# Four output half rows straight from the accumulator instead of two, with the accumulator copied out by two engines and the last left group moved behind the last right product

## The chip, the cores and the metric

The kernel runs on 1 core of one Trainium2 chip. The metric is the device time of one execution in microseconds. Before the change it is 201.84 us, the median of 3 runs (201.77 to 201.89).

## The reference

Two stages follow each other. A slot attention over 8 batches and 8 heads makes `x`; a soft mixture of 8 experts with 4 slots each (32 slots in all) makes the output, 4608 rows of 512 columns.

```python
logits = x @ phi                       # 4608 x 32
d = softmax(logits, over rows)         # dispatch
slot_input = d.T @ x                   # 32 slots
for e in range(8):                     # 4 slots an expert
    slot_out[e] = relu(slot_input[e] @ w1[e]) @ w2[e]
c = softmax(logits, over slots)        # combine
out = c @ slot_out                     # 4608 x 512
```

The change touches only the last two lines: how `slot_out` is gathered from its accumulator, and how `out` is multiplied, evicted and stored.

## The kernel before

Every operation of the kernel is entered with `add(engine, cost, ...)` in a plan. `Plan.order` then plays the plan through with the given costs and issues the operations in the order in which they would start; so the order of each engine's instructions comes from those costs, from the tiles' dependencies and from the `after` lists.

**The expert weights.** `expert_in` (line 1385) multiplies the slot inputs by `w1`, `hidden` applies the relu (line 1401, ScalarE) and transposes (line 1410, TensorE; line 1416, VectorE), `mult` (line 1431) multiplies by `w2`. The second product is kept in two accumulators, one for each half of the 512 output columns: the left half in `kvbank`, the right half in `scbank`. In each, four groups of 32 partitions hold four partial sums. The last four half experts' `w2` come in quarter loads of 256 KB, left columns first (`tail_out`). The four left products of these tails (`tail_mult(0, n)`) therefore end before the four right ones (`tail_mult(1, n)`).

**The slot sums.** `slot_sums(d)` copies the accumulator of half `d` to `accs` (tile name `cS`, line 1349; VectorE for the left half, ScalarE for the right one), multiplies it by `rep`, which adds the four partial sums (line 1357), and splits the sum in a high part (ScalarE cast, line 1364) and a low part (VectorE subtraction, line 1369): the two halves of `sr`.

**Output rows.** The combine weights `c` are transposed to `cT`, also as high and low parts. `out_mult` (line 1603) makes 128 output rows of a batch pair with two matmuls of 64 rows, one for each part. `direct` (line 1587) needs no slot sums: it multiplies `accs` itself by `c4`, four copies of the transposed weights one under the other, in one full fp32 matmul. The copies in `c4` are made by ScalarE (line 1553), in the middle of `slots(0)`. Each product goes to one of four PSUM banks and is evicted to SBUF, by ScalarE (line 1579) or VectorE (line 1580).

**Order of the end.** The left half is written out by four groups of three half rows while the right products still run; `RIGHT = (-1, 1, 2, 2)` says behind which left group each right tail product stands. Then come the right slot sums, four right groups, and at last 24 products of the full 512 columns, stored as 3, 3, 9 and 9 rows. All stores and loads are issued by SyncE (stores on line 1616), 16 stores in this order: left half rows 0, 1, 2 one by one, left groups 1, 2, 3, the same six for the right half, and the four wide stores.

Of the kernel before, what the change touches and what calls it, by code (L numbers as in the profile page):

```python
# [16 lines left out]
PE, DVE, ACT, POOL, SP = range(5)  # L17
# [3 lines left out]
class Plan:  # L21
# [24 lines left out]
    def add(self, eng, cost, fn, r=(), w=(), also=(), pri=None, dma=0.0, slack=0.0, after=()):  # L46
        cost, ni = cost if isinstance(cost, tuple) else (cost, 4)
        i = len(self.ops)
        deps = set()
        tiles = {}  # L50
        for x in r:
            for key in x:
                tiles[key[0]] = None
                if key in self.last_w:
                    deps.add(self.last_w[key])
        for x in w:
            for key in x:
                tiles[key[0]] = None
                if key in self.last_w:
                    deps.add(self.last_w[key])  # L60
                deps.update(self.reads.get(key, ()))
        for x in w:
            for key in x:
                self.last_w[key] = i
                self.reads[key] = []
        for x in r:
            for key in x:
                self.reads.setdefault(key, []).append(i)
        deps.discard(i)
        deps.update(after)  # L70
        tiles = [t for t in tiles if t.pool is not None]
        for t in tiles:
            t.users += 1
        need = tiles + [t for t in also if t not in tiles]
        if pri is None:
            pri = self.phase[0]
            self.phase[0] += self.phase[1]
        self.ops.append((eng, cost, fn, deps, pri, dma, tiles, need, slack, ni))
        return i
# [170 lines left out]
def dve(n):  # L250
    return 0.15 + n / 960.0


def act(n, psum=True):
    return (0.16 if psum else 0.19) + n / 1200.0
# [15 lines left out]
def kernel(  # L271
# [30 lines left out]
    P = 128  # L302
# [40 lines left out]
    Q_SZ, QT_SZ = C * J * D, C * J * D // 2  # L343
    KP_W = R * (P + Y)
    EX_SZ = PC + JN
    ARENA = 44288
    arena = const.tile([P, ARENA], F32, name="arena")

    CT_ALL = NBP * J * P
    TOP = 10 ** 6  # L350
    top_pool = ExitStack()
    qtile = top_pool.enter_context(tc.tile_pool(name="top", bufs=1)).tile([P, CT_ALL], F32, name="top")
# [943 lines left out]
        [qtile[:, i * W_SZ: i * W_SZ + W_SZ] for i in range(2)],  # L1296
        [(TOP + i * W_SZ, W_SZ) for i in range(2)], [qs],
    )
    ND = 2
    late_tiles = []  # L1300

    def late(x, off, n):
# [35 lines left out]

    pacc = [b_kv.tile(), b_s2.tile()]
    HD = DM // 2  # L1340
    accs = acs.tile().split(2)
    sr = keep("sr", [P, 2, DM], dtype=F32R, parts=2)
    so = [b_l.tile(), Tile(ap=kvbank[:, 1])]

    def slot_sums(d, middle=lambda: None):
        x = slice(d * HD, d * HD + HD)
        add(
            *((ACT, act(HD)) if d else (DVE, dve(HD))),
            lambda: (nc.scalar.copy if d else nc.vector.tensor_copy)(
                accs.ap[:, x], pacc[d].ap[:, 0, :HD]  # L1350
            ),
            r=[pacc[d]], w=[accs.part(d)],
        )
        y = middle()
        z = add(
            PE, 0.5,
            lambda: nc.tensor.matmul(
                so[d].ap[:, :HD], rep.rearrange("p a n -> p (a n)"), accs.ap[:, x],
                start=True, stop=True,
            ),  # L1360
            r=[accs.part(d), rep_b], w=[so[d]], after=[y] if y is not None else (),
        )
        add(
            ACT, act(HD), lambda: nc.scalar.copy(sr.ap[:, 0, x], so[d].ap[:, :HD]),
            r=[so[d]], w=[sr.part(d)],
        )
        add(
            DVE, dve(HD),
            lambda: nc.vector.tensor_tensor(
                sr.ap[:, 1, x], so[d].ap[:, :HD], sr.ap[:, 0, x].bitcast(F32), op=ALU.subtract  # L1370
            ),
            r=[so[d], sr.part(d)], w=[sr.part(d)],
        )
        return z
# [123 lines left out]
    def slots(bp):  # L1498
        Lb = L[bp]
        lv = Lb.ap.rearrange("p (j n) -> p j n", j=J)  # L1500
        mx, sm = cmxs.tile(), csms.tile()
        cxb, cx = Lb, lambda: lv
        bc = lambda t: t.ap.unsqueeze(2).to_broadcast([P, J, NS])
        add(
            DVE, dve(JN), lambda: nc.vector.tensor_reduce(mx.ap, lv, axis=AX.X, op=ALU.max),
            r=[Lb, SIM], w=[mx],
        )
        add(
            DVE, dve(JN),
            lambda: nc.vector.tensor_tensor(cx(), lv, bc(mx), op=ALU.subtract),  # L1510
            r=[mx], w=[cxb],
        )
        add(ACT, act(JN, False), lambda: nc.scalar.activation(cx(), cx(), AF.Exp), r=[cxb], w=[cxb])

        def f():
            nc.vector.tensor_reduce(sm.ap, cx(), axis=AX.X, op=ALU.add)
            nc.vector.tensor_scalar(sm.ap, sm.ap, EPS, None, op0=ALU.add)
            nc.vector.reciprocal(sm.ap, sm.ap)
            nc.vector.tensor_mul(cx(), cx(), bc(sm))

        add(DVE, 1.2, f, r=[cxb], w=[sm, cxb])
        x, ct = xs.tile().split(2), cTs.tile().split(2)
        cT[bp] = ct
        for a in range(2):
            js = range(a, J, 2)
            n, h = len(js) * P, HALF * a

            def f(a=a, h=h, n=n):
                o = x.ap[h: h + NS, :n].rearrange("m (j q p) -> m q j p", q=4, p=NS)
                for i in range(4):  # L1530
                    nc.vector.transpose(o[:, i], cx()[NS * i: NS * i + NS, a::2, :])

            add(DVE, 4 * dve(n // 4), f, r=[cxb], w=[x.part(a)])
            add(
                ACT, act(n, False),
                lambda h=h, n=n: nc.scalar.copy(ct.ap[h: h + NS, :n], x.ap[h: h + NS, :n]),  # L1536
                r=[x.part(a)], w=[ct.part(a)],
            )
            add(
                POOL, pool_tt(n),  # L1540
                lambda h=h, n=n: nc.gpsimd.tensor_tensor(  # L1541
                    ct.ap[h + NS: h + HALF, :n], x.ap[h: h + NS, :n],
                    ct.ap[h: h + NS, :n].bitcast(F32), op=ALU.subtract,
                ),
                r=[x.part(a), ct.part(a)], w=[ct.part(a)],
            )
        if bp == 0:

            def f():
                for i in range(ND):  # L1550
                    h = HALF * i
                    for y in range(0, P, NS):
                        nc.scalar.copy(c4.ap[y: y + NS, i * P: i * P + P], x.ap[h: h + NS, :P])

            add(ACT, 4 * ND * act(P, False), f, r=[x], w=[c4])

# [24 lines left out]
        )  # L1581

    def direct(d, i, after=()):
        po, ot, s = b_o.tile(), half[0], slice(d * HD, d * HD + HD)
        x = add(
            PE, 0.45,
            lambda: nc.tensor.matmul(
                po.ap[:, :HD], c4.ap[:, i * P: i * P + P], accs.ap[:, s],
                start=True, stop=True,
            ),  # L1590
            r=[accs.part(d), c4], w=[po], also=[ot], after=after,
        )
        add(
            *evict(lambda: ot.ap[:, i * DM + s.start: i * DM + s.stop], po, HD, i % 2 == d),
            r=[po], w=[ot.part(G * d + i)],
        )
        store(0, i, s, ot, [ot.part(G * d + i)], i)
        return x

    def out_mult(bp, j, po, x):  # L1600
# [19 lines left out]
            r=r, dma=P * n * (x.stop - x.start) * 4 / (DMA_RATE if x.stop - x.start == DM else HALF_RATE),  # L1620
        )

    def half_group(d, n, single=False):
        (bp, j0), ot, x = groups[n], half[n], slice(d * HD, d * HD + HD)
        for i in range(ND if single else 0, G):
            po = b_o.tile()
            z = add(
                PE, 0.22, lambda po=po, j=j0 + i: out_mult(bp, j, po, x),
                r=[sr.part(d), cT[bp]], w=[po], also=[ot],
            )  # L1630
            y = i * DM + d * HD
            add(
                *evict(lambda y=y: ot.ap[:, y: y + HD], po, HD, (j0 + i) % 2),
                r=[po], w=[ot.part(G * d + i)],
            )
            if single:
                store(bp, j0 + i, x, ot, [ot.part(G * d + i)], i)
        if not single:
            store(bp, j0, x, ot, [ot.part(G * d + i) for i in range(G)])
        return z  # L1640

    outv = out.rearrange("(p j) d -> p j d", j=J)
    z = slot_sums(0)
    for i in range(ND):
        z = direct(0, i, [z])
    for n in range(-1, NA):
        if n >= 0:
            z = half_group(0, n, n == 0)
        for m in range(NT):
            if RIGHT[m] == n:  # L1650
                tail_mult(1, m, [z])
        if RIGHT[NT - 1] == n:
            y = slot_sums(1)
            for i in range(ND):
                y = direct(1, i, [y])
    for n in range(NA):
        half_group(1, n, n == 0)
    for bp, j0, n in ((1, 3, 3), (1, 6, 3), (2, 0, 9), (3, 0, 9)):
        ot = (ots if n == G else big[n]).tile().split(n)
        for i in range(n):  # L1660
# [42 lines left out]
```

## Time and profile before

| what | value |
|---|---|
| median of 3 runs | 201.84 us |
| the profiled execution | 201.61 us |
| its span, first to last instruction | 199.8 us |
| TensorE busy | 168.4 us (84%), 2595 matmul records |
| VectorE busy | 140.7 us (70%) |
| ScalarE busy | 74.0 us (37%) |
| GpSimd busy | 95.5 us (48%) |
| DMA | 76.47 MB, mean 383 GB/s |

The rest of the execution, 1.8 us, lies outside of the span. The page shows the span in 40 slices of 5 us: DMA is at nine tenths or more in nearly all of them, and moves 396 to 431 GB/s in most of the later ones; in the seven slices from 160 us on it moves 313, 337, 303, 238, 369, 417 and 413 GB/s, and 295 in the last. The granted TensorE clock is at its upper level until 193 us. An fp32 matmul has two records in the trace, so one `tail_mult` of four matmuls is shown as x8, and one `direct` as x2; one `out_mult` is x2 as well.

### The profile page before, as it was taken

The page shows a single profiled execution, that of the slowest core. Times are in us where ns is not written, and L with a number is a line of the kernel's source. Part 1 is how long each engine was busy: PE and PEld are TensorE (multiplying, and loading weights), DVE is VectorE, ACT ScalarE, POOL GpSimd, SP SyncE. Part 2 cuts the span into 40 slices and gives each one's busy share as a digit, 9 for nine tenths or more (in the row PEclk, how much of TensorE's full clock was granted, in tenths as well). Part 3 has the DMA queues.
Part 4 walks back from the last instruction along what each step waited for, and adds up shares of the span by engine and source line. Part 5 has one row for each costly group of instructions (what it writes and reads, how often), then busy time and mean ns, then how long its engine had stood idle before and what let it go on. Part 6 is the DMA issues. An engine that isn't in the chain of part 4 may idle for free.

```text
span 199.8 us, 6056 instructions
## 1 busy us (share of the span) xinstructions
PE 168.4 (84%) x2595; PEld 107.3 (54%) x2595; DVE 140.7 (70%) x264; ACT 74.0 (37%) x188; POOL 95.5 (48%) x92
## 2 busy tenths in 40 slices
PE   7989747978699899887999889799999988989800
PEld 6777534636457477554666357465555642566400
DVE  7831740699897899999899997378999800658800
ACT  2022314536351655516554243110239400456500
POOL 7199303589993894979964276100006960000000
PEclk9999997899969999999999999999999999999985
DMA  6999999999999999999999999999999999979996
GB/s 199 365 392 394 382 384 390 380 389 380 404 379 390 388 382 401 386 389 402 417 423 392 423 421 418 417 421 431 430 430 426 396 313 337 303 238 369 417 413 295
DMA packets 29098, 76.47 MB, mean 383 GB/s; under 512 B 1936, under 2 KB 13200, under 8 KB 25744
## 3 DMA queue, kind: packets, MB, share of 16 engines
q1 hardware_dynamic: 29072, 76.09, 99.6%
q8 instruction: 20, 0.33, 0.7%
q14 instruction: 6, 0.05, 0.1%
HBM read 66.65 MB, written 9.44 MB: 381 GB/s over the span
## 4 chain that ended last, share of the span: by engine, by line
PE 38%; DMA 20%; DVE 13%; POOL 12%; issue 4%; SPq 4%; ACT 2%; POOLq 0%; DVEq 0%
DMA arena<-in_moe_w_dram 12%; DMA arena<-in_v_dram 8%; PE bank L1603 7%; PE scbank L813 6%; PE kvbank L704 5%; SPq L502 4%; PE bank L882 4%; POOL arena L848 3%; PE bank L1385 3%; POOL arena L871 3%; POOL arena L669 3%; POOL arena L648 3%; PE bank L1010 2%; DVE arena L606 2%; DVE arena L827 2%
## 5 line engine op out<-in xcount | busy, mean ns | idle before, releaser
L648 POOL TENSOR_TENSOR arena<-arena 128x1152 f32<-128x1152 f32 x8 | 21.0, 2632 | 17.5 <-ACT arena L641 15.2
L591 DVE STREAM_TRANSPOSE arena<-top 128x1152 f32<-128x1152 f32 x16 | 21.6, 1354 | 8.4 <-DMA top<-in_q_dram 8.4
L704 PE MATMUL kvbank<-arena 64*32 64x128 f32 x1152 | 21.2, 279 | 6.2 <-issue 2.9
L520 PE MATMUL kvbank<-ones 128*128 128x256 f32 x82 | 23.8, 427 | 2.4 <-ACT arena L728 1.3
L813 PE MATMUL scbank<-arena 64*64 64x288 f32 x256 | 23.8, 445 | 2.2 <-DVE arena L827 2.1
L669 POOL TENSOR_TENSOR arena<-arena 128x128 f32<-128x128 f32 (+2 forms) x32 | 23.4, 730 | 3.2 <-ACT arena L657 1.3
L1541 POOL TENSOR_TENSOR cT<-cS,cT 32x640 fp32r<-32x640 f32 (+1 forms) x8 | 11.3, 1412 | 26.2 <-ACT cT L1536 25.8
L871 POOL TENSOR_TENSOR arena<-arena,ssm 128x576 f32<-128x576 f32 x16 | 18.3, 1151 | 9.5 <-DVE ssm L867 7.9
L704 PEld LDWEIGHTS kvbank<-arena 64*32 64x32 f32 x1152 | 16.6, 107 | 10.8 <-issue 5.8
L848 POOL TENSOR_TENSOR arena<-arena,smx 128x576 f32<-128x576 f32 x16 | 18.4, 1150 | 7.6 <-DVE smx L843 7.6
L882 PE MATMUL bank<-arena 128*128 128x288 f32 x64 | 18.8, 425 | 1.3 <-DVE arena L874 0.8
L606 DVE TENSOR_REDUCE arena<-arena 128x128 f32<-128x1152 f32 x8 | 17.1, 2148 | 3.5 <-DMA arena<-in_phi_dram 3.5
L520 PEld LDWEIGHTS kvbank<-ones 128*128 128x128 f32 x82 | 16.0, 210 | 6.1 <-ACT arena L728 1.7
L1580 DVE COPY arena<-bank 128x256 f32<-128x256 f32 (+1 forms) x27 | 13.8, 548 | 3.6 <-PE bank L1603 3.1
L827 DVE STREAM_TRANSPOSE arena<-scbank 128x576 f32<-128x576 f32 x16 | 12.2, 765 | 5.4 <-PE scbank L813 5.4
L813 PEld LDWEIGHTS scbank<-arena 64*64 64x64 f32 x256 | 9.8, 139 | 10.1 <-DVE arena L827 3.6
L853 ACT ACTIVATE arena<-arena 128x576 f32<-128x576 f32 x16 | 10.9, 684 | 11.2 <-POOL arena L848 11.0
L882 PEld LDWEIGHTS bank<-arena 128*128 128x128 f32 x64 | 11.2, 189 | 6.4 <-DVE arena L874 1.9
L1603 PE MATMUL bank<-sr,cT 64*128 64x512 f32 (+1 forms) x88 | 14.6, 378 | 0.0
L1385 PE MATMUL bank<-arena,SIM 128*32 128x256 f32 x224 | 13.3, 392 | 0.2 <-DVE SIM L1264 0.2
L874 DVE STREAM_TRANSPOSE arena<-arena 128x576 f32<-128x576 f32 x16 | 11.9, 756 | 1.5 <-POOL arena L871 1.5
L1431 PE MATMUL kvbank<-arena 128*32 128x256 f32 x128 | 11.6, 382 | 1.2 <-DMA arena<-in_moe_w_dram 0.8
(135 smaller groups left out, 258.8 us busy)
## 6 DMA issues: line engine op xcount, KB each, us to landing
arena<-in_moe_w_dram SPq DMA_DIRECT2D x18, 1024.0 KB, 13.6
top<-in_q_dram SPq DMA_DIRECT2D x8, 1152.0 KB, 12.6
arena<-in_k_dram SPq DMA_DIRECT2D x8, 1152.0 KB, 10.1
arena<-in_v_dram SPq DMA_DIRECT2D x8, 1152.0 KB, 12.5
arena<-in_moe_w_dram SPq DMA_DIRECT2D x4, 2048.0 KB, 15.3
arena<-in_phi_dram SPq DMA_DIRECT2D x8, 576.0 KB, 7.0
out_dram<-arena SPq DMA_DIRECT2D x2, 2304.0 KB, 7.8
arena<-in_moe_w_dram SPq DMA_DIRECT2D x16, 256.0 KB, 5.7
```

Of the source, the lines that this page charges most:

```text
L520: lambda: nc.tensor.matmul(warm.ap, ones, ones.unsqueeze(1).to_broadcast([P, 2, P]), start=True, stop=True,),
L591: lambda: nc.vector.transpose(qT.ap.rearrange("p (i u y) -> p u i y", i=2, y=Y), qt.ap[:, h * QT_SZ: h * QT_SZ + QT_SZ].rearrange("p (u i ...
L606: lambda: nc.vector.tensor_reduce(mx.ap[:, c0:c1], ph().rearrange("p c j m -> p c m j"), axis=AX.X, op=ALU.max),
L648: lambda: nc.gpsimd.tensor_tensor(ph(), ph(), mb.ap[:, c0:c1].unsqueeze(2).to_broadcast([P, c1 - c0, J, M]), op=ALU.subtract,),
L669: plus = lambda o, x, y: nc.gpsimd.tensor_tensor(o, x, y, op=ALU.add)
L704: nc.tensor.matmul(acc.ap[M * c: M * c + M, a, : 2 * D], ph()[h0: h0 + HALF, c, j, :], kv()[h0: h0 + HALF, :, c, j * D: j * D + D], start= ...
L813: nc.tensor.matmul(scb.ap[HALF * g: HALF * g + HALF, a, :JY], pair[g].kd.ap[h0: h0 + HALF, i, c].rearrange("p r m -> p (r m)"), pair[g].qT ...
L848: lambda: nc.gpsimd.tensor_tensor(exv(), exv(), bc(mx), op=ALU.subtract),
L871: lambda: nc.gpsimd.tensor_tensor(exv(), exv(), bc(sm), op=ALU.mult),
L882: nc.tensor.matmul(lp.ap[:, :JY], vpb.ap[:, h, :], aT.ap[:, a * JY: (a + 1) * JY], start=(h == 0), stop=(h == H - 1),)
L1385: nc.tensor.matmul(hb.ap[NS * j: NS * j + NS, :256], SIM.ap[:, 2 * i + c, NS * e: NS * e + NS], wv[:, c].rearrange("p (x j t) -> p x j t", ...
L1603: nc.tensor.matmul(po.ap[:, : x.stop - x.start], cT[bp].ap[y: y + HALF, j // 2 * P: j // 2 * P + P], sr.ap[y: y + HALF, t, x], start=(t == 0),
```

## The change

Four half rows (`ND = 4`) of each half come from `direct`. Rows 0 to 2 of the left half are still stored one by one; the fourth is the first row of group 1 and leaves with its group. The groups then make the products that are left: none in group 0, two in group 1, three in each of groups 2 and 3. In each half two of the `direct` products are placed ahead of the `rep` product (`middle`), and two behind it. The copy out of the accumulator is cut in two pieces of 128 columns, one for VectorE and one for ScalarE. The products of left group 3 get the last right tail product in their `after` list. `c4` holds four blocks, so ScalarE makes 16 small copies for it where it made 8, and the arena is 256 columns smaller.

```diff
-    ARENA = 44288
+    ARENA = 44032
+    ND = 4
...
-        add(
-            *((ACT, act(HD)) if d else (DVE, dve(HD))),
-            lambda: (nc.scalar.copy if d else nc.vector.tensor_copy)(
-                accs.ap[:, x], pacc[d].ap[:, 0, :HD]
-            ),
-            r=[pacc[d]], w=[accs.part(d)],
-        )
+        for i, (eng, cost, copy) in enumerate((
+            (DVE, dve(P), nc.vector.tensor_copy), (ACT, act(P), nc.scalar.copy),
+        )):
+            z = slice(i * P, i * P + P)
+            add(
+                eng, cost,
+                lambda copy=copy, z=z: copy(accs.ap[:, x][:, z], pacc[d].ap[:, 0, z]),
+                r=[pacc[d]], w=[accs.part(2 * d + i)],
+            )
...
             def f():
                 for i in range(ND):
-                    h = HALF * i
+                    h, z = HALF * (i % 2), i // 2 * P
                     for y in range(0, P, NS):
-                        nc.scalar.copy(c4.ap[y: y + NS, i * P: i * P + P], x.ap[h: h + NS, :P])
+                        nc.scalar.copy(c4.ap[y: y + NS, i * P: i * P + P], x.ap[h: h + NS, z: z + P])
...
-    def half_group(d, n, single=False):
-        for i in range(ND if single else 0, G):
+    def half_group(d, n, after=()):
+        for i in range(max(0, min(G, ND - G * n)), G):
...
+    firsts = (2, 2)
+
+    def directs(d):
+        y = []
+        for i in range(firsts[d]):
+            y = [direct(d, i, y)]
+        return y[0]
+
-    z = slot_sums(0)
-    for i in range(ND):
-        z = direct(0, i, [z])
+    z = [slot_sums(0, lambda: directs(0))]
+    for i in range(firsts[0], ND):
+        z = [direct(0, i, z)]
+    z = z[0]
+    last = []
     for n in range(-1, NA):
         if n >= 0:
-            z = half_group(0, n, n == 0)
+            z = half_group(0, n, last) or z
         for m in range(NT):
             if RIGHT[m] == n:
-                tail_mult(1, m, [z])
-        if RIGHT[NT - 1] == n:
-            y = slot_sums(1)
-            for i in range(ND):
-                y = direct(1, i, [y])
+                w = tail_mult(1, m, [z])
+                if m == NT - 1:
+                    last = [w]
+                    y = [slot_sums(1, lambda: directs(1))]
+                    for i in range(firsts[1], ND):
+                        y = [direct(1, i, y)]
```

TensorE from the third right tail product on, before: `scbank<-arena` is a right tail product, `kvbank<-cS,rep` the right slot sums, `bank<-cS` a `direct`, `bank<-sr,cT` a product of the groups.

```order
L1431 MATMUL scbank<-arena 32x256 x4
L1603 MATMUL bank_64<-sr,cT 128x256 x2
L1603 MATMUL bank_62<-sr,cT 128x256 x2
L1603 MATMUL bank_63<-sr,cT 128x256 x2
L1431 MATMUL scbank<-arena 32x256 x4
L1357 MATMUL kvbank<-cS,rep 128x256
L1587 MATMUL bank_65<-cS 128x256
L1587 MATMUL bank_64<-cS 128x256
L1603 MATMUL bank_62<-sr,cT 128x256 x2
```

The same place in the changed program.

```order
L1433 MATMUL scbank<-arena 32x256 x8
L1607 MATMUL bank_62<-sr,cT 128x256 x2
L1607 MATMUL bank_65<-sr,cT 128x256 x2
L1607 MATMUL bank_63<-sr,cT 128x256 x2
L1590 MATMUL bank_64<-cS 128x256
L1590 MATMUL bank_62<-cS 128x256
L1359 MATMUL kvbank<-cS,rep 128x256
L1590 MATMUL bank_65<-cS 128x256
L1590 MATMUL bank_63<-cS 128x256
L1607 MATMUL bank_64<-sr,cT 128x256 x2
```

The third left group stands behind the last right tail product, and two `direct` products stand between it and the slot sums, two more behind them. Up to the first wide product eight right group products follow, where ten stood before.

ScalarE around the copy of the right accumulator, before, with the semaphores that each instruction waits for (`PE_49` is TensorE's, `DVE_49` VectorE's).

```order
L1579 COPY arena<-bank_62 128x256 [waits PE_49]
L1349 COPY cS<-scbank 128x256 [waits PE_49]
L1364 CAST sr<-kvbank 128x256 [waits DVE_49,PE_49]
L1579 COPY arena<-bank_64 128x256 [waits PE_49]
L1579 COPY arena<-bank_63 128x256 [waits PE_49]
```

The same place in the changed program.

```order
L1353 COPY cS<-scbank 128x128 [waits DVE_49]
L1581 COPY arena<-bank_65 128x256 [waits PE_49]
L1581 COPY arena<-bank_64 128x256 [waits PE_49]
L1366 CAST sr<-kvbank 128x256 [waits PE_49]
L1581 COPY arena<-bank_65 128x256 [waits PE_49]
```

ScalarE's copy is 128 columns wide and waits for VectorE's semaphore in place of TensorE's; VectorE's own copy of the other 128 columns waits for TensorE. Two evictions moved in between the copy and the cast.

## Rows read from the trace of the kernel before

**Rows 1.** The chain of waits, its last part: start us, us, what

```profile
162.21 5.71 DMA arena<-in_moe_w_dram
...
168.65 0.44 DVE cS L1349
...
169.13 0.70 PE bank L1357 x2
169.83 0.86 PE bank L1587 x4
170.69 0.57 PE scbank L1431 x8
171.26 0.67 PE bank L1603 x8
...
174.40 0.61 PE scbank L1431 x8
...
175.03 0.38 ACT cS L1349
...
175.46 0.70 PE kvbank L1357 x2
176.16 0.86 PE bank L1587 x4
177.02 2.48 PE bank L1603 x19
...
179.52 9.81 PE bank L1603 x47
```

**Rows 2.** SyncE's timeline, three of the 16 stores: start us, us issuing

```profile
177.46 0.34 SPq L1616 DMA_DIRECT2D out_dram<-arena  x1
...
186.50 0.33 SPq L1616 DMA_DIRECT2D out_dram<-arena  x1
...
190.11 0.33 SPq L1616 DMA_DIRECT2D out_dram<-arena  x1
```

**Rows 3.** Line 1616, stretches 186 to 187 us and 190 to 191 us

```profile
DMA to landing us min/median/max: 6.9/6.9/6.9
...
DMA to landing us min/median/max: 8.8/8.8/8.8
```

**Rows 4.** Table by stretches: busy us of the engines, TensorE clock, DMA share, GB/s

```profile
177.00:178.30 1.30, 1.30 (x13) 1.00 (x12) 1.06 (x4) 0.98 (x3) 0.00 (x0) 1.00 0.14 48
...
180.00:187.00 7.00, 7.00 (x38) 4.48 (x36) 5.85 (x11) 4.59 (x8) 0.00 (x0) 1.00 1.03 384
...
187.00:187.25 0.25, 0.25 (x3) 0.17 (x4) 0.25 (x2) 0.00 (x0) 0.00 (x0) 1.00 0.09 25
...
187.50:198.10 10.60, 1.82 (x10) 0.80 (x6) 2.11 (x4) 1.51 (x3) 0.00 (x0) 0.78 0.98 417
```

**Rows 5.** Groups by line and shape, copies of 128 columns from PSUM: busy, mean ns

```profile
L641 ACT COPY arena<-bank 128x128 f32<-128x128 f32 x8 | 2.1, 265 | 19.9 <-PE bank L630 19.8
...
L1416 DVE COPY arena<-bank 128x128 f32<-128x128 f32 x2 | 0.5, 265 | 0.0
```

**Rows 6.** Timeline, ScalarE from 150 us and TensorE at 162 us

```profile
150.61 2.46 ACT L1553 COPY cS<-cS 32x128 f32<-32x128 f32 x8
...
153.09 0.38 ACT L1401 ACTIVATE arena<-bank 128x256 f32<-128x256 f32 x1
...
162.23 0.64 PE L1431 MATMUL kvbank<-arena 128*32 128x256 f32 x8 [0.79 <-DMA arena<-in_moe_w_dram]
```

**Rows 7.** Timeline of ScalarE and VectorE from 176 us

```profile
176.19 0.37 ACT L1364 CAST sr<-kvbank 128x256 fp32r<-128x256 f32 x1 [0.79 <-PE kvbank L1357]
...
176.60 0.42 DVE L1369 TENSOR_TENSOR sr<-kvbank,sr 128x256 fp32r<-128x256 f32 x1 [1.64 <-ACT sr L1364]
176.94 3.18 DVE L1580 COPY arena<-bank 128x256 f32<-128x256 f32 x7
```

More of the change, by code (lines that the diff above doesn't have):

```diff
@@ L345 @@
     EX_SZ = PC + JN
-    ARENA = 44288
+    ARENA = 44032
     arena = const.tile([P, ARENA], F32, name="arena")
-    CT_ALL = NBP * J * P
+    ND = 4
+    CT_ALL = NBP * J * P + (ND - 2) * P
     TOP = 10 ** 6
@@ L1298 @@
     )
-    ND = 2
     late_tiles = []
@@ L1340 @@
     HD = DM // 2
-    accs = acs.tile().split(2)
+    accs = acs.tile().split(4)
     sr = keep("sr", [P, 2, DM], dtype=F32R, parts=2)
@@ L1360, in slot_sums @@
             ),
-            r=[accs.part(d), rep_b], w=[so[d]], after=[y] if y is not None else (),
+            r=[accs.part(2 * d), accs.part(2 * d + 1), rep_b], w=[so[d]], after=[y] if y is not None else (),
         )
@@ L1583, in direct @@
     def direct(d, i, after=()):
-        po, ot, s = b_o.tile(), half[0], slice(d * HD, d * HD + HD)
+        g, k, s = i // G, i % G, slice(d * HD, d * HD + HD)
+        po, ot = b_o.tile(), half[g]
         x = add(
@@ L1590, in direct @@
             ),
-            r=[accs.part(d), c4], w=[po], also=[ot], after=after,
+            r=[accs.part(2 * d), accs.part(2 * d + 1), c4], w=[po], also=[ot], after=after,
         )
         add(
-            *evict(lambda: ot.ap[:, i * DM + s.start: i * DM + s.stop], po, HD, i % 2 == d),
-            r=[po], w=[ot.part(G * d + i)],
-        )
-        store(0, i, s, ot, [ot.part(G * d + i)], i)
+            *evict(lambda: ot.ap[:, k * DM + s.start: k * DM + s.stop], po, HD, i % 2 == 0),
+            r=[po], w=[ot.part(G * d + k)],
+        )
+        if g == 0:
+            store(0, i, s, ot, [ot.part(G * d + i)], i)
         return x
@@ L1621, in store @@
         )
-    def half_group(d, n, single=False):
-        (bp, j0), ot, x = groups[n], half[n], slice(d * HD, d * HD + HD)
-        for i in range(ND if single else 0, G):
+    def half_group(d, n, after=()):
+        z, (bp, j0), ot, x = None, groups[n], half[n], slice(d * HD, d * HD + HD)
+        for i in range(max(0, min(G, ND - G * n)), G):
             po = b_o.tile()
@@ L1628, in half_group @@
                 PE, 0.22, lambda po=po, j=j0 + i: out_mult(bp, j, po, x),
-                r=[sr.part(d), cT[bp]], w=[po], also=[ot],
+                r=[sr.part(d), cT[bp]], w=[po], also=[ot], after=after,
             )
@@ L1635, in half_group @@
             )
-            if single:
-                store(bp, j0 + i, x, ot, [ot.part(G * d + i)], i)
-        if not single:
+        if n:
             store(bp, j0, x, ot, [ot.part(G * d + i) for i in range(G)])
@@ L1642 @@
     outv = out.rearrange("(p j) d -> p j d", j=J)
-    z = slot_sums(0)
-    for i in range(ND):
-        z = direct(0, i, [z])
+    firsts = (2, 2)
[9 more added lines that the diff above has]
+    last = []
     for n in range(-1, NA):
         if n >= 0:
-            z = half_group(0, n, n == 0)
+            z = half_group(0, n, last) or z
         for m in range(NT):
             if RIGHT[m] == n:
-                tail_mult(1, m, [z])
-        if RIGHT[NT - 1] == n:
-            y = slot_sums(1)
-            for i in range(ND):
-                y = direct(1, i, [y])
+                w = tail_mult(1, m, [z])
[4 more added lines that the diff above has]
+                        y = [direct(1, i, y)]
     for n in range(NA):
-        half_group(1, n, n == 0)
+        half_group(1, n)
     for bp, j0, n in ((1, 3, 3), (1, 6, 3), (2, 0, 9), (3, 0, 9)):
```

## Prediction

> **What bounds the kernel now.** I read the chain of waits first [rows 1]. Up to 168 us it hangs on the loads of the expert weights; from the left copy at 168.65 us it is a chain of computing: copy, slot sums (`rep`), `direct` products, right tail products, left groups, and after the right copy at 175.03 us the same for the right half, until the 24 wide products begin at 179.52 us. They and their evictions take 9.81 us and end it at 190.04 us.
>
> The chain as listed stops there, but the span goes on to 199.8 us, so I went on to the stores. The first of the two 9-row stores is issued at 186.50 us, the second at 190.11 us [rows 2]; they land 6.9 and 8.8 us later [rows 3], at 193.4 and 198.9 us, 5.5 us apart. From 187.5 to 198.1 us the DMA engines are at 0.98 with 417 GB/s [rows 4], so the second store lies right behind the first, and when it is issued doesn't matter: 190.11 us is 3.3 us ahead of the first one's landing. What matters is the first. The DMA engines are full from 180 to 187 us, but in the quarter microsecond ahead of its data their share is 0.09 [rows 4]: they had run dry. So the end is the issue of the first 9-row store plus 12.4 us (198.9 less 186.50), and that issue hangs on the 15th wide eviction. Any shift of the wide stage's start is a shift of the end. The idle DMA time earlier, 177.0 to 178.3 us at 0.14 [rows 4], is time in which bytes could go out, but getting them out sooner only makes the engines run dry sooner.
>
> **The change part by part, on the way to the wide stage.**
>
> The copy. Before it takes 0.44 us with its start on VectorE (left), 0.38 on ScalarE (right) [rows 1]. Now it is two copies of 128 columns, 0.265 us each on either engine [rows 5]. The program's order has ScalarE's half wait for VectorE's semaphore, so they stand one behind the other: 0.265 + 0.04 + 0.265 = 0.57 us, 0.04 being the gap from one engine's end to the next one's start in the chain (175.41 to 175.46). That is 0.13 us more on the left and 0.19 on the right. Side by side it would be about 0.29. I take the serial price, because the wait stands in the program.
>
> The Trainium skill, "PSUM — Partial Sum Buffer", section "PSUM bank collisions raise a hardware error", gives a reason for such a wait: two engines may not access one bank at the same time on the same partitions, two reads included. Both halves of an accumulator lie in one bank. By that rule the copy costs 0.57 us, without it 0.29; no row here shows two engines in one bank at once.
>
> The left half, to the last right tail product's end. Before, from the start of `rep` at 169.13 us: `rep` with its start 0.70, two `direct` 0.86, four tail products of 0.57, three groups (four, three and three products) of 0.67 each [rows 1] (tails and groups repeat; a row or two of each stands there): 0.70 + 0.86 + 2.28 + 2.01 = 5.85, to 174.98; the trace has 175.01. Now one fp32 product with its start 0.70, four more at 0.43, the same four tails, a group of two and a group of three. The group of two is not in the trace: between half of a group of four (0.34) and the group of three (0.67) I take 0.43, nearer to the half. 0.70 + 1.72 + 2.28 + 0.43 + 0.67 = 5.80. With a start 0.13 later the last tail product ends 0.08 later, at 175.1 us. The high and low parts of the left sum come later too (two `direct` stand ahead of `rep`), but two `direct` and a tail product, 1.43 us, stand between `rep` and the first product that needs them, against 0.86 us for cast and subtraction (from 176.16 to 177.02 on the right).
>
> The right half. Before: tail ends 175.01, copy, `rep` ends 176.16, cast and subtraction end 177.02 [rows 1, 7]; the two `direct` fill just these 0.86 us. Now: group 3's three products (0.67) run while the accumulator is copied (0.02 + 0.57), so both are done at about 175.75. This is the cover that the move buys: some 0.5 us of TensorE's wait. But then come 0.05 of start, `direct` 0.70, `direct` 0.43, `rep` 0.43: `rep` ends at 177.36, and cast and subtraction at 178.2, 1.2 us later than now. The two `direct` behind `rep` lie beside cast and subtraction and cost nothing there.
>
> Behind the sums eight products are left instead of ten. Ten take 2.48 us [rows 1], 0.25 each, with evictions; eight take 1.98. So the wide stage begins at 180.2 us instead of 179.52: 0.7 later. I don't let the pace change: both engines evict, four banks rotate as before. If the engines caught up by their own pace (VectorE's seven in 3.18 us [rows 7] hold pauses), up to 0.3 of it would come back; if the first products had to wait for the fourth `direct`'s bank, up to 0.25 would be added.
>
> Stores. Their number, sizes and order on SyncE are unchanged. The first right one goes out about 0.5 us sooner than 177.46 (`direct` at 176.5, eviction 0.37), left group 3's some 1.2 us later, since its products now follow the tail. Neither gates anything: the DMA engines catch up before 187 us as they do now, and then wait longer for the first 9-row store. The wide stage itself has the same 24 products, 24 evictions, banks and alternation.
>
> Earlier edits at nothing. Eight more copies for `c4` keep ScalarE 2.46 us longer at 153.07 us, ahead of the relu at 153.09 [rows 6]; the program's order moves the transposes behind it past five more `w2` products on TensorE, and the first product that needs their result comes some 3 us after that. The cover is the weight stream: TensorE waits 0.79 us for a load at 162.23 [rows 6] anyway, and the last left tail product hangs on a load. If it were gone, up to 2.5 us would show. Some waits of weight loads for their buffers moved by a place or two in SyncE's queue with the smaller arena; the loads are queued deep, so nothing, at most 0.4 either way.
>
> **Sum.** 0.13 − 0.05 + (178.2 − 177.02 − 0.08) − 0.50 = 0.7 us (the 1.2 of the right half holds the left half's 0.08). On the profiled execution: 201.61 + 0.7 = 202.3 us, span 200.5. The median of the runs is 0.23 above that execution: 202.5 us. Own range, with the catching up and the extra wait: +0.4 to +0.95, 202.2 to 202.8.
>
> **Rivals.**
>
> *No measurable change.* The sums come late, but the eight products behind them run at the evictors' own pace: five of them on VectorE at about 0.34 each when they stand in line, 1.7 us instead of 1.98, and wide evictions that begin with both engines free make up another 0.1. For it: TensorE is the one that waits for banks in this stretch. Against: the 3.18 us of VectorE for seven copies are the pace with the same four banks. +0.3, 202.1 us. The copies running side by side after all would take 0.28 off each half and leave +0.1, 201.9; the wait in the program speaks against it.
>
> *Faster.* VectorE's queue is what sets 176.6 to 180.1: a subtraction and seven copies with hardly a pause [rows 7]. After the change three of VectorE's evictions (two of group 3, one `direct`) stand ahead of the subtraction, six behind it. If VectorE never starved, it would go from the last tail product's end through 0.27 + 9 × 0.42 + 0.42 = 4.5 us, to 179.6 us instead of 180.1: −0.5 us, 201.3 us. It decides by whether the subtraction starts by 177 us as now. Against it: the cast that the subtraction waits for hangs on `rep`, which now stands behind two more `direct`.
>
> *Much slower.* The longer `c4` copies or a weight load that waits a place too early reach the weight stream: some 0.5 us more at the left copy, +1.2, 203.0 us. Against it: the DMA-bound wait at 162.23 us.
>
> **How the numbers follow.** My forecast 0.53, no measurable change 0.29, faster 0.12, much slower 0.06. A measurement here tells about 0.2% (0.4 us) from no change. The forecast's own range touches +0.4 only at its edge; some 0.02 of it falls inside. Faster 0.12, same 0.31, slower 0.57. For 8 in 10 the range goes from 201.6 (leaving out most of the faster case) to 202.95 us.
>
> **What would show it.** In the profile after: ScalarE's 128-column copy starts behind VectorE's end, not beside it; the last right tail product ends near 175.1 us; the right `rep` near 177.4 instead of 176.16; the first wide product near 180.2; the first 9-row store near 187.2, with a DMA share near zero for almost a microsecond ahead of it, and the last landing 12.4 us later. I am wrong if the wide stage starts by 179.6 us, if the left copy isn't at 168.6 us, or if the end doesn't follow the first 9-row store.

## The result, and the profile after

The changed kernel takes 203.26 us (median of 20 runs, 202.58 to 205.07); the kernel before, run beside it, 201.90 us (20 runs, 201.50 to 203.11). The ratio is 1.0073 [1.0056, 1.0090]: slower by 1.36 us, about twice the 0.7 us that was predicted. The profiled execution is the shortest of the 20, 202.58 us with a span of 200.8 us, so it shows only a part of the loss: 0.97 us of the 1.36.

The chain of waits of the changed kernel, its last part (start us, us, what), to be laid beside [rows 1]:

```profile
162.33 5.99 DMA arena<-in_moe_w_dram
...
169.05 0.30 DVE cS L1353
...
169.38 0.28 ACT cS L1353
...
169.69 1.13 PE bank L1590 x4
170.82 0.43 PE bank L1359 x2
171.26 0.86 PE bank L1590 x4
...
174.35 1.00 PE scbank L1433 x16
175.35 0.67 PE bank L1607 x5
...
176.06 1.13 PE bank L1590 x4
177.20 0.43 PE kvbank L1359 x2
177.63 0.86 PE bank L1590 x4
178.49 11.81 PE bank L1607 x60
```

The left copy starts at 169.05 us, 0.40 later than before, though nothing of the change stands ahead of it but the loads and the `c4` copies. From there on the tail looks as forecast: the two copies stand one behind the other (0.30 and 0.28 us), the last right tail product ends at 175.35 us, the right `rep` at 177.63, and the wide products, taken as 9.81 us as in [rows 1], begin at 190.30 - 9.81 = 180.49 us. With 0.40 taken off these are 174.95, 177.23 and 180.09 us; forecast were 175.1, 177.36 and 180.2. The tail, from the left copy to the end of the wide products, has grown from 20.68 to 21.25 us: 0.57 us.

SyncE's timeline of the two 9-row stores (start us, us issuing), and the view of line 1620 in the two stretches around them, answer [rows 2] and [rows 3]:

```profile
187.45 0.33 SPq L1620 DMA_DIRECT2D out_dram<-arena  x1
...
191.08 0.33 SPq L1620 DMA_DIRECT2D out_dram<-arena  x1
```

```profile
DMA to landing us min/median/max: 6.9/6.9/6.9
...
DMA to landing us min/median/max: 8.8/8.8/8.8
```

The end is 191.08 + 8.8 = 199.9 us, 12.4 us after the first 9-row issue, as before. The table by stretches (the last two columns are DMA share and GB/s) has the engines dry ahead of that store's data and full behind it, as [rows 4]:

```profile
187.90:188.15 0.25, 0.25 (x4) 0.11 (x3) 0.25 (x2) 0.04 (x1) 0.00 (x0) 1.00 0.00 0
188.45:199.10 10.65, 1.83 (x10) 0.80 (x6) 2.12 (x4) 1.52 (x3) 0.00 (x0) 0.68 0.98 415
```

What the forecast did not have lies more than 60 us ahead of the left copy. The same table for 103 to 105.5 us, the kernel before first, the changed one second:

```profile
103.00:105.50 2.50, 2.50 (x63) 2.29 (x64) 2.46 (x6) 1.67 (x6) 1.40 (x2) 1.00 1.02 403
```

```profile
103.00:105.50 2.50, 2.50 (x64) 2.30 (x64) 2.46 (x6) 1.71 (x6) 1.15 (x1) 1.00 0.58 200
```

Half of the bytes are missing for 2.5 us, in a stream that is full from 95 us on. The reason stands in SyncE's order with its waits. Rows of before, then of after; the 40th DMA is the second row of each (counted from 1, as below):

```
L502 DMA arena<-in_moe_w_dram 128x2048 [waits DMAHW6_49,PE_49]
L502 DMA arena<-in_moe_w_dram 128x2048 [waits DMAHW7_49]
L502 DMA arena<-in_moe_w_dram 128x2048 [waits PE_49,DMAHW0_49,Activation_49,Pool_49]
```

```
L503 DMA arena<-in_moe_w_dram 128x2048 [waits DMAHW6_49]
L503 DMA arena<-in_moe_w_dram 128x2048 [waits PE_49,DMAHW7_49,Activation_49,Pool_49]
L503 DMA arena<-in_moe_w_dram 128x2048 [waits DMAHW0_49]
```

The weight buffers lie at the arena's end, 2048 columns each. With an arena 256 columns shorter they all move, and one that was free early now reaches into an area that the attention stage gives up late. So load 40 takes over the wait that load 41 had. The lines of its issue (ns of issuing, first and last start) and its landing, before (loads 39 and 40) and after (load 40):

```profile
L502 SPq DMA_DIRECT2D arena<-in_moe_w_dram x2: 424/863/1302, 91.2 to 92.6; - x2
...
DMA to landing us min/median/max: 15.3/15.9/16.5
```

```profile
L503 SPq DMA_DIRECT2D arena<-in_moe_w_dram x1: 327/327/327, 104.1 to 104.1; - x1
...
DMA to landing us min/median/max: 5.0/5.0/5.0
```

Issued at 92.55 us before, at 104.11 after; landed at 109.07 and 109.13. Eleven and a half microseconds later in, and only 0.06 later out. The trace's 16 landing events of a load say why: before, the first of the 16 DMA engines ends load 40 at 105.39 us and the last at 109.07. The last one decides, and after the change it had work left from load 39 until 106.81 us (taking it that the same engine is last in both loads, which the trace does not tell). The other engines went idle until the gap to it had closed: in the changed kernel load 40 lands between 108.44 and 109.13. Nothing is lost yet, but what had been 3.7 us between the engines is now 0.7.

Further on, the last landing is later than before by 1.23 us at load 42, by 0.08 at load 57, and by 0.41 at load 65, whose landing the left copy waits for. So the 0.40 of the left copy is that of load 65; why the delay shrinks and comes back on the way is not shown.

### The profile page after: what moved, and what is told of

It is laid out like the page before. It is cut to its first block, busy times and chain, and to the rows that moved or that the text cites. A ratio compares the mean times of both kernels' runs of the same rounds, so it can differ in the third digit from the quotient of the medians.

```text
span 200.8 us, 6068 instructions
## 1 busy us (share of the span) xinstructions
PE 168.8 (84%) x2595; PEld 108.4 (54%) x2595; DVE 141.5 (70%) x265; ACT 76.7 (38%) x197; POOL 95.5 (48%) x92
## 4 chain that ended last, share of the span: by engine, by line
PE 37%; DMA 21%; DVE 13%; POOL 12%; issue 4%; SPq 4%; ACT 2%; POOLq 0%; DVEq 0%
DMA arena<-in_moe_w_dram 13%; DMA arena<-in_v_dram 8%; PE bank L1607 7%; PE scbank L814 6%; PE kvbank L705 4%; SPq L503 4%; PE bank L883 4%; POOL arena L849 3%; POOL arena L872 3%; POOL arena L670 3%; PE bank L1387 3%; POOL arena L649 3%; PE bank L1011 2%; DVE arena L607 2%; PE bank L1590 2%
## 5 line engine op out<-in xcount | busy, mean ns | idle before, releaser
L521 PE MATMUL kvbank<-ones 128*128 128x256 f32 x82 | 23.3, 420 | 2.4 <-ACT arena L729 1.3
L849 POOL TENSOR_TENSOR arena<-arena,smx 128x576 f32<-128x576 f32 x16 | 18.4, 1152 | 7.7 <-DVE smx L844 7.7
L1607 PE MATMUL bank<-sr,cT 64*128 64x512 f32 (+1 forms) x80 | 13.8, 384 | 0.0
L1581 ACT COPY arena<-bank 128x512 f32<-128x512 f32 (+1 forms) x21 | 10.1, 485 | 7.4 <-PE bank L1607 4.7
```

The lines of the kernel that those rows point to most:

```text
L521: lambda: nc.tensor.matmul(warm.ap, ones, ones.unsqueeze(1).to_broadcast([P, 2, P]), start=True, stop=True,),
L849: lambda: nc.gpsimd.tensor_tensor(exv(), exv(), bc(mx), op=ALU.subtract),
L1607: nc.tensor.matmul(po.ap[:, : x.stop - x.start], cT[bp].ap[y: y + HALF, j // 2 * P: j // 2 * P + P], sr.ap[y: y + HALF, t, x], start=(t == 0),
```

## The experiments

Theory: the loss has two parts, the tail (0.57 us) and the load that the smaller arena holds back. Rival: all of it is the tail, or the longer `c4` copies. The first run of the small arena, the whole change with the loads as before, the one copy and the moved group ran beside 23 runs of the kernel before (median 201.85 us); the second run of the small arena, the four behind and the held loads beside 27 (201.93 us); the four looks at the end beside one (202.06 us).

**The smaller arena alone.** The kernel before with one line changed:

```diff
-    ARENA = 44288
+    ARENA = 44032
```

> The kernel before with one number of the change: the arena is 256 columns smaller, so every weight tile lies 256 columns lower; the end of the kernel stands as before. Theory A (loads): the weight load that must wait for four engines' release of its buffer is now one place earlier in SyncE's queue; it is issued near 104.1 us instead of 92.6, the DMA engines run dry at 103 to 105.5 us (share near 0.58 instead of 1.02), and the weight stream has no reserve against the slowest DMA engine. The whole kernel is 0.4 to 1.2 us slower than before, with runs that spread over more than 1 us; the left copy comes after 168.65 us in the profile. Rival B (tail): the loads cost nothing, the size was off in the tail alone: 0.0 us (within 0.2).

Measured: 202.2 to 203.7 us in five executions, ratio 1.0058 [1.0038, 1.0078]. Most of the loss, with no instruction of the tail changed. A sixth, the profiled one, took 379 us with TensorE busy for 361.1 us instead of 168.4 (the 128x256 product of line 520 took 823 ns instead of 427); it says nothing about loads, so the kernel was run again.

> The kernel before with the arena of 44032 columns alone, run again, for a profile of it that can be read and beside the two kernels with held buffers. By the theory of the loads: 203.0 us again (202.7 to 203.3), load 40 issued near 104 us, DMA share near 0.58 from 103 to 105.5 us, the left copy 0.4 to 1.3 us later than 168.65, and from the left copy to the issue of the first 9-row store 17.85 us as before. Rival (it was chance, or the tail): within 0.3 us of before.

Measured: 202.98 us (10 runs, 201.87 to 203.88), ratio 1.0040 [1.0011, 1.0069]. The profiled execution is the shortest, 201.87 us: load 40 issued at 103.71, share 0.64 from 103 to 105.5 us, left copy 168.92 (0.27 later than before, where 0.4 or more was expected), and 17.84 us from it to the first 9-row issue, before 17.85. That rules out the tail. But the ten times fall into two groups, four up to 202.5, near before's 201.93, and six from 202.96 on; a single profile of the lower group can't show the rest.

**The whole change, but with the loads as before.** `c4` is put into a free gap of the arena, which keeps its 44288 columns:

```diff
-    ARENA = 44032
+    ARENA = 44288
...
+    c4s = over([ND * P], 1)
```

> The whole change, but the two more blocks of the transposed weights lie in a gap of the arena that the weight tiles leave free, so the arena keeps its size and SyncE's loads wait for the same releases as before. Theory A: DMA share near 1.0 at 103 to 105.5 us again, left copy near 168.65 us, and what is left is the tail's price: +0.6 us against before (0.4 to 0.8), first 9-row store near 187.1 us, runs as close together as before's. Rival B: still +1.3 us.

Measured: 202.33 us (12 runs, 201.96 to 203.87), ratio 1.0015 [1.0003, 1.0028]. By the ratio that is 0.1 to 0.6 us more than before: rival B falls, and the theory's 0.4 to 0.8 is met at most in its lower part. The share from 103 to 105.5 us is 1.02 again. With the arena's first ratio, 0.58%, the two add up to the change's 0.73%; with its second, 0.40%, to 0.55%, just under the change's interval. The tail as traced (left copy 170.36, first 9-row issue 188.78) is 18.42 us against 17.85, as in the changed kernel.

This profile is of the longest of the twelve, and its left copy is 1.71 us later than before although load 40 waits for nothing new. It is late from well ahead of that load: load 31 is issued at 79.08 us, before at 76.72. So long executions have more than one source, and the held load is not behind all of them.

**As that, with one copy instead of two.** `slot_sums` copies 256 columns on one engine again.

> As the run before it, with the accumulator copied by one instruction of 256 columns as before the change (VectorE left, ScalarE right). Theory A: the two 128-column copies stand in a row and cost 0.13 to 0.19 us more in each half, so about 0.3 us comes back: +0.3 us against before (0.1 to 0.45). Rival C (the copies overlap or are hidden by group 3's products): no difference from the run before it, +0.6.

Measured: 202.14 us (11 runs), ratio 1.0010 [1.0000, 1.0019]; tail 187.02 - 168.91 = 18.11 us. By these two traces the cut copy costs 0.31 us over both halves; the times (0.15% and 0.10%) point the same way, but their intervals overlap.

**As that, with all four `direct` products behind `rep`:**

```diff
-    firsts = (2, 2)
+    firsts = (0, 0)
```

> Loads as before, one undivided copy, four direct products in each half as in the change, but all four behind rep; the last left group still moved behind the last right tail product. It differs from the kernel with one copy (202.14 us) only in that no direct product stands ahead of rep. Theory (the place ahead of rep is what costs, since cast and subtraction then start 0.86 us later): on the right rep ends 0.86 sooner and two direct products more stand between it and the eight products: 0.2 to 0.5 us less than that kernel, 201.65 to 201.95 us. Rival (it is their number: four products of 0.43 in place of two of 0.43 and two of 0.25): the same as that kernel, 202.0 to 202.3 us.

Measured: 202.10 us (11 runs), ratio 1.0008 [0.9999, 1.0017]: the same, and here the theory fell. The chain of the kernel with two `direct` ahead, then of the one with four behind:

```profile
175.72 1.06 PE bank L1586 x4
178.07 11.77 PE bank L1603 x61
```

```profile
176.32 1.73 PE bank L1586 x8
178.04 11.81 PE bank L1603 x62
```

They end at 189.84 and 189.85 us. A later `rep` costs nothing here, because TensorE has `direct` products to do either way; what counts is the sum of what it must do between the copy and the end.

**The last left group moved, and nearly nothing else.** Two `direct` in each half, behind `rep`, one copy, loads as before. Two small things of the change stay in it: `c4` lies in the gap of the arena, as in the three kernels above, and the two engines that evict the right `direct` products have changed places.

```diff
-    ND = 4
+    ND = 2
...
-    firsts = (2, 2)
+    firsts = (0, 0)
```

> Of the change only the last left group behind the last right tail product: two half rows straight from the accumulator, behind the slot sums, one copy, loads as before. Theory A: group 3's products cover the copy's wait, and no direct product stands ahead of the slot sums: the right sums come some 0.6 us earlier and the wide stage begins some 0.85 us earlier (first 9-row store near 185.7 us). As the right stores begin a microsecond earlier too, the DMA engines keep up: -0.6 to -0.85 us against before, 201.1 us. Rival D (bytes): the DMA engines have 187.0 us as their own end of the backlog, so no more than 0.25 us comes: 201.65 us. Rival B: 0 or slower, as moving the group itself was what cost.

Measured: 200.96 us (6 runs, 200.86 to 201.74), ratio 0.9961 [0.9948, 0.9973]: faster than both kernels, by about as much as theory A had it. The profiled execution is the longest of the six, with its left copy at 169.38, 0.73 us later than before; so only the stretches behind that copy are read from it. Its chain around the right copy:

```profile
173.91 1.11 PE scbank L1429 x16
175.02 0.66 PE bank L1603 x6
175.69 0.63 PE kvbank L1355 x2
176.31 0.86 PE bank L1586 x4
177.18 12.14 PE bank L1603 x63
```

The left group's three products (175.02, 0.66) fill the time of the copy, for which TensorE idled from 175.01 to 175.46 us in [rows 1]. The tail is 186.47 - 169.38 = 17.09 us, 0.76 shorter than before. So, by one trace each, the tail's 0.57 is made of -0.76 for the moved group, +0.31 for the cut copy, and the rest, 1.02, for four `direct` in place of two. The last agrees with products counted (0.98): on the right two `direct` of 0.43 replace two products of 0.25 (+0.36), on the left 0.86 are added and a group of four becomes one of two (0.67 to 0.43, +0.62).

**One load held, two loads held.** The kernel before, arena and all; one or two of the three early weight buffers are kept out of the plan until the late area is released:

```diff
+    ws.hold = (34048,)
```

> The kernel before, arena and all, with one thing changed: one of the three weight buffers that are free early is kept out of the plan until the early stage's area is released. So one w1 load, number 40 in SyncE's queue, waits for TensorE, ScalarE and GpSimd as number 41 did before, and 41 finds its buffer free. Nothing else moves up to that place. Theory (this one load's wait is the cost of the smaller arena): as with the smaller arena alone, 0.8 to 1.3 us more than before, 202.7 to 203.2 us, and a DMA share near 0.58 instead of 1.02 from 103 to 105.5 us. Rival (the smaller arena costs by the other waits that moved with it, such as the first 2 MB w2 load): within 0.3 us of before, 201.6 to 202.2, though the load is issued late.

Measured: 202.22 us (12 runs, 201.77 to 203.71), ratio 1.0030 [1.0010, 1.0050]. Between theory and rival: eight executions from 201.77 to 202.30, near the rival, and four from 203.24 to 203.71, where the theory had it. The profile is of the lower group (202.30 us) and has a share of 0.64 from 103 to 105.5 us.

> As the kernel with one buffer held, with a second one held as well: loads 39 and 40 of SyncE's queue both wait for the early stage. Each is 1 MB, some 2.5 us at 420 GB/s. Theory (the queue of loads runs dry, and what one load in flight covers is lost at once): the DMA engines stand idle for some 2.5 us longer than with one load held, so 2.5 to 3.7 us more than before, 204.4 to 205.5 us. Rival (the loads have reserve later on, and the cost with one held lies elsewhere): no more than with one held, under 203.2 us.

Measured: 204.54 us (4 runs, 204.20 to 205.32), ratio 1.0136 [1.0113, 1.0159]: +2.6 us, by the theory. The stretches from 100.5 us and the chain:

```profile
100.50:103.00 2.50, 2.02 (x22) 1.10 (x18) 2.40 (x5) 1.68 (x6) 1.77 (x2) 1.00 0.40 164
103.00:105.50 2.50, 2.50 (x64) 2.29 (x63) 2.46 (x6) 1.67 (x6) 1.28 (x2) 1.00 0.23 46
```

```profile
143.62 21.23 DMA arena<-in_moe_w_dram
164.91 5.92 DMA arena<-in_moe_w_dram
```

The last load of the chain is issued at 164.91 us, before at 162.21 [rows 1], and with one load held, in the execution of 202.30 us, at 162.78. So the first load held cost 0.57 us there and the second 2.13 more (2.3 by the medians), where 1 MB is 2.5 us of the stream. The first was mostly paid out of the gap between the engines, the second nearly in full.

**Looks at longer executions.** The changed kernel and the small arena, twice each, to see what the upper group has.

> The changed kernel, one more execution with a profile, since its 20 times run from 202.6 to 205.1 us and the one profile is of the shortest. If this one is 203.2 us or longer: theory of the held load: what is added comes after load 40, because the slowest of the 16 DMA engines was less far behind the others when the load was held, so that it runs dry too; load 39's last landing would lie under 3 us behind its first (3.7 before), load 41's last landing 0.5 us or more behind 111.6, and the left copy about as much later as the time is longer. Rival: the addition lies ahead of load 39 (the early stage) or behind the left copy, with load 39 as skewed as before. If it is 202.9 us or shorter it should look like the first profile.

> As the look before it, the same kernel and the same two readings: an addition that begins with load 40 and a small skew of load 39 by the theory of the held load, an addition ahead of it or behind the left copy by the rival.

Measured: 203.23 and 203.71 us. The theory's reason is not borne out: load 39 lands over 3.4 and 3.3 us, less than the 3.7 of the first profile but above the mark of 3. The addition does begin where the theory has it. Load 39 lands 0.4 us earlier than in the first profile, load 40 is 0.13 and 0.92 us later, load 41 lands at 112.46 and 112.51 us instead of 111.61, and the left copy starts at 169.71 and 170.17 instead of 169.05: 0.66 and 1.12 later, in executions that are 0.65 and 1.13 longer. (In the second look load 42 is 0.65 later; the rest of the 1.12 is added behind it.) From the left copy to the first 9-row issue it is 18.4 us in all three. Load 41 in the first profile and in the first look (ns of issuing; us to landing):

```profile
L503 SPq DMA_DIRECT2D arena<-in_moe_w_dram x1: 432/432/432, 104.5 to 104.5; - x1
...
DMA to landing us min/median/max: 7.1/7.1/7.1
```

```profile
L503 SPq DMA_DIRECT2D arena<-in_moe_w_dram x1: 1556/1556/1556, 104.4 to 104.4; - x1
...
DMA to landing us min/median/max: 8.0/8.0/8.0
```

The stretch from 108 to 112 us in the same two executions:

```profile
108.00:112.00 4.00, 4.00 (x38) 2.50 (x34) 3.94 (x5) 1.68 (x4) 1.85 (x2) 1.00 1.01 426
```

```profile
108.00:112.00 4.00, 4.00 (x39) 2.51 (x34) 3.94 (x5) 1.68 (x4) 2.14 (x2) 1.00 0.94 324
```

In the longer execution SyncE takes 1.56 us to issue load 41 (1.39 in the second look), and the engines run dry a second time: 102 GB/s less over 4 us are 0.41 MB, 0.96 us of the stream. In the three short ones of this arrangement (the first profile, and 201.87 us twice with the small arena) load 41 takes 0.43 us, and the long issue (1.34, 1.38, 1.15 us) falls on load 42. Before, there is such an issue too (load 39, 1.30 us), but it costs nothing: it is over at 92.50 us, and no engine is done with load 38 before 100.42.

The DMA records of the traces tell more of the long issue. Besides the data, each trace has 20 transfers of 16 KB of kind "instruction" on queue q8 (number, MB and share on the page of the kernel before):

```profile
q8 instruction: 20, 0.33, 0.7%
```

Each takes about 1 us. In the twelve traces of ordinary length 31 load issues between 70 and 140 us take 0.7 us or more, and 29 of them end 0.36 to 0.59 us behind the end of such a transfer. In the two looks it begins at 104.55 and 104.45 us, and load 41, issued at 104.43 and 104.50, is held until 105.99 and 105.89. In the three short executions it begins at 104.64, 104.51 and 104.58, load 41 (104.48, 104.08, 104.39) gets out in time, and load 42 is the one held. So in these five a tenth or two of a microsecond between the burst of issues and that transfer goes with which load is held. This is read from the traces; no experiment moved the transfer.

> The kernel before with the smaller arena alone, one more execution with a profile; its times run from 201.9 to 203.9 us. If it is 202.9 us or longer: by the theory of the held load the addition begins with load 40 or 41 and load 39's last landing lies under 3 us behind its first; by the rival it lies elsewhere.

> As the look before it, the same kernel and the same two readings.

Measured: 201.87 us, of the lower group and like the profile above; and 240 us with a mean granted TensorE clock of 0.65 (0.96 in the first profile after), which says nothing about loads. So no longer execution of the small arena has a usable profile.

## Why the prediction was wrong

Point by point, by its own steps:

- **The copy.** Right: serial, 0.60 and 0.60 us with the gap, forecast 0.57. The traces with two copies and with one put its price at 0.31 us over both halves; 0.13 + 0.19 were forecast.
- **Left half, right half, eight products.** Right within 0.15 us: +0.57 in the trace, +0.55 to the first 9-row issue, against 0.7. The argument behind it was partly wrong: the 1.2 us by which `rep` is late were charged and the eight products credited, which comes out as the sum of TensorE's work but reads as if the place of `rep` cost something. The kernel with four behind shows that it doesn't. One row was misread without harm to the sum: the 9.81 us are the wide products alone, to 189.33 us, and the last eviction comes on top.
- **Stores.** Right: the end is the first 9-row issue plus 12.4 us, with a share of 0.00 ahead of its data.
- **Early edits at nothing.** This is the step that failed. "The loads are queued deep, so nothing, at most 0.4 either way" holds for the shortest executions (0.40 at the left copy), not for the median. The queue was not deep at load 40: with that load held, the engines ran dry (share 0.58). The arena alone costs 0.4 to 0.6% by its two comparisons (0.8 to 1.2 us), more than the tail; the wait of one load alone costs 0.30% (0.6 us). The sum then is 0.57 plus 0.8 to 1.2, or 1.4 to 1.8 us; 1.36 was measured, with an interval of 1.1 to 1.8. The prediction's own sign of being wrong, a left copy that isn't at 168.6 us, came true.
- **The `c4` copies at nothing.** Not shown either way, but small: with the loads as before and 16 copies, the left copy starts at 168.91 us (one copy) and 168.87 (four behind), 0.26 and 0.22 after before's 168.65. Before's profile is itself 0.23 us shorter than its median, and 168.92 was also seen with the small arena and 8 copies.

The rival "much slower" had the right mechanism, a load that waits a place too early, and 203.0 us; it got a chance of 0.06. What spoke against it was read the wrong way round: TensorE's wait for a load at 162.23 us [rows 6] is no cover for the stream, it shows that the stream is what is waited for. The same text had the chain hanging on the loads up to 168 us. A delay of TensorE or ScalarE hides behind that wait; a delay of a load can't. How deep the queue was could also have been read: load 41 was issued at 104.14 us, while load 39's first engine had ended at 102.91.

Shown: that the arena's size costs most of the loss, that one load's wait alone costs a good part of that (1.0030 [1.0010, 1.0050]), that a second such load costs nearly its full time, and where two longer executions of the changed kernel lose theirs. Left open: whether the held load is all that the small arena costs, since the kernel with one load held loses less (1.0030 against 1.0058 and 1.0040) with intervals that overlap. The changed kernel issues two more loads over 3 us later than before, load 47 (116.32 us, before 112.27) and the first 2 MB load of `w2` (136.04, before 132.43), but no engine is done with the load ahead of them before 123.36 and 140.78 us, so by the traces neither wait emptied the queue. Open too is why a load's issue is held while an instruction transfer runs, and what makes the long executions that the kernel before has as well (up to 204.03 us).

## What to carry to other kernels

A change in a buffer's size or place can change the waits of every load behind it: compare the order of the load queue with its waits row by row, and where the chain hangs on the loads, price a moved wait from its issue time against the landing of the load ahead of it. Here the stream's reserve was what its slowest engine had left, and once that was used, a long issue on SyncE showed in the time. In a tail where one engine is always busy, add up its work; here the order mattered only where it filled an idle stretch, and the one such edit here (the moved group) is worth 0.4% nearly by itself.

## What was not expected of the hardware

The 16 DMA engines that share a load do not end it together: before the hold, the last landed 3.7 us behind the first (load 40), more than a whole 1 MB load of 2.5 us, and a pause of the stream evens them out to 0.7 us. The Trainium skill, "DMA: Bandwidth & Descriptors", section "Latency and other measured facts", says that two of the 16 engines are usually slower than the others; its guess at a cause concerns only transfers issued by GpSimd. These loads are issued by SyncE, so that guess does not cover the gap here, and no run here shows which engines land last. In most bursts of loads one issue on SyncE took 1.0 to 1.6 us where the others took 0.3 to 0.5, and between 70 and 140 us 29 of the 31 long ones ended just behind a 16 KB instruction transfer.
